# Two attentions in one program: starting with A's first group chunk by chunk, lending idle score banks, and fillers

## The chip, the cores and the metric

The kernel runs on one core of one Trainium2 chip. The metric is the device time of one execution in microseconds (us); lower is better. Engines: PE is the matmul engine (PEld its weight loads), ACT the activation engine, DVE the vector engine, POOL the general one, SP the one that issues DMA. "Span" is the time from the first to the last instruction in a trace; the timed figure of the same execution is 1.3 to 3.6 us longer in the runs here.

## The reference

Two independent attention blocks, each with 2048 rows, width 1024 and 32 heads of 32, side by side in the output.

```
A:  q, k, v = x @ wqkv ; out_A = softmax(q k^T / sqrt(32)) v @ wo          # full 2048 x 2048
B:  4 segments of 512 rows; in each: causal softmax attention inside the segment,
    plus a memory read  phi(q) M / (phi(q) z + 1e-6), mixed by g = sigmoid(beta);
    then M += phi(k)^T v, z += sum phi(k)            # phi(t) = t+1 if t>0 else exp(t)
out = concat(out_A, out_B)
```

The work comes in 8 groups of 4 heads. Per group, A has 8 items (256 queries against 2048 keys; 16 exponentials on ACT, each over two banks, 128 x 1024). B has 32 items (4 segments x 8 groups; 6 exponentials each). Together 1024 + 192 = 1216 score exponentials.

## The kernel before

A planner in Python writes every engine's instruction list at build time. It keeps an estimated clock, gives score matmuls precedence whenever score banks are free, and fits "side" work (projections, output projections, memory updates) and the multiplications by V ("PV") into the gaps of PE. The chip then runs that fixed order with semaphores. PSUM has 8 banks: 0 to 5 for scores, 6 for the PV sums, 7 for side work (6 also, until the first PV).

```
SLOTS = [(0, 1), (2, 3), (4, 5)]      # score banks in pairs
OLB = 6 ; PROJ = [7]
PACE = 200 ; LEAD = 3 ; SLOPE = 0.55  # when A's next group is prepared; when B's item is taken before A's
# ...
def loads(self):                      # B's weights and 4 tiles of B_x first
    self.load_WB(0, 0)
    for k in range(4):
        tile_in(16 + k, self.B_x[0][P * k:P * k + P, :])
        # ...
    self.load_WA(0, 0)
    for k in range(16):
        tile_in(k, self.A_x[0][P * k:P * k + P, :])
        # ...
# a_prep(g), group 0: K of all four 512-column chunks, then Q of the first, and only then scores
    for c in range(4):
        if g == 0:
            yield from self.turn([...4 tiles of x, transposed on PE, copied out by DVE and ACT in turn...])
        yield from proj(0, c)                     # K
    # ...
        yield from proj(1, 0)                     # Q of chunk 0
        # ...
        self.events.add(("sA", g, c))             # scores may start
        if c == 0:
            for v in range(4):
                yield from proj_V(v)
# schedule(): fillers on a free side bank, gap of 0.3 us, until 45 us
    if now < 45 and (RING - 1) not in self.ring_busy and not self.pos_ring and gap >= 0.3 and bank is not None:
        R.op("PE", lambda e, bank=bank: e.matmul(...), cost=MM)
```

The exponentials go to a ring of 20 tiles (10 exponentials) from which PV reads.

Of the kernel before, what the change touches and what calls it, by code (L numbers as in the profile page):

```python
# [11 lines left out]
P = 128  # L12
S = 2048
D = 1024
NI = D // P
NG = 8
# [210 lines left out]
PACE = 200  # L227
LEAD = 3
SLOPE = 0.55
STICK = True  # L230
NQ = S // 256


class Kernel:
# [69 lines left out]
    def alloc(self):  # L304
# [36 lines left out]
        self.beta = sb("beta", [P, 8])  # L341
# [28 lines left out]
    def stage(self, k):  # L370

        if k < 16:
            return self.OTA[:, k // 2, 1024 * (k % 2):1024 * (k % 2) + 1024], [("OTA", k // 2, 4 * (k % 2) + c) for c in range(4)]
        k -= 16
        flat = self.OTB[0][:, :, :].rearrange("p j n -> p (j n)")
        return flat[:, 1024 * k:1024 * k + 1024], [("OTB", 0, 2 * k), ("OTB", 0, 2 * k + 1)]

    def loads(self):
        R = self.R
        nc = self.nc  # L380

        def tile_in(k, src):
            dst, keys = self.stage(k)
            R.dma(lambda e: e.dma_start(dst, src), w=keys, issue=0.5)  # L384
        self.load_WB(0, 0)
        for k in range(4):
            tile_in(16 + k, self.B_x[0][P * k:P * k + P, :])
            if k == 1:
                self.load_WB(1, 0)
        self.events.add(("xB", 0))  # L390
        self.load_WA(0, 0)
        for k in range(16):
            tile_in(k, self.A_x[0][P * k:P * k + P, :])
            if k == 3:
                for h in range(4):
                    src = bass.AP(tensor=self.B_beta.tensor, offset=self.B_beta.offset + h, ap=[[0, 32], [4, NG]])

                    def f(e, h=h, src=src):
                        with nc.allow_non_contiguous_dma(reason="tiny beta broadcast"):
                            return e.dma_start(self.beta[32 * h:32 * h + 32, 0:NG], src)  # L400
                    R.dma(f, w=[("beta", h)], issue=0.5, mb=0.01)
            if k == 7:
                self.load_WA(1, 0)
                self.load_WB(2, 0)
        self.load_WA(2, 0)

    def late_loads(self):
        yield ("pos", 40)
        self.load_xB(1)
        self.R.dma(lambda e: e.dma_start(self.WoB[:, :, :], self.B_wo.rearrange("(j p) n -> p j n", p=P)), w=["WoB"], mb=2.0)  # L410
        self.events.add("WoB")

    def turn(self, tiles):

        R = self.R
        for n, (k, dst, dkeys) in enumerate(tiles):
            src, keys = self.stage(k)
            bank = yield ("bank",)
            yield ("pe", self.ready(keys))

            def f(e, src=src, bank=bank):
                for i in range(NI):
                    ins = e.transpose(self.psb[:, bank, P * i:P * i + P], src[:, P * i:P * i + P], self.ident[:, :])  # L423
                return ins
            R.op("PE", f, r=keys + ["ident"], w=[("ps", bank)], cost=0.9)
            pv = self.psb[:, bank, :].rearrange("p (i n) -> p i n", i=NI)
            if n % 2:
                op = R.op("ACT", lambda e, dst=dst, pv=pv: e.activation(dst, pv, ACTF.Copy), r=[("ps", bank)], w=dkeys, cost=1.1)  # L428
            else:
                op = R.op("DVE", lambda e, dst=dst, pv=pv: e.tensor_copy(dst, pv), r=[("ps", bank)], w=dkeys, cost=1.2)  # L430
            self.bank_release(bank, op)

# [29 lines left out]
    def gates(self):  # L462

        R = self.R
        rb = [("beta", h) for h in range(4)]
        gA, gB = self.gcol[:, 0, :], self.gcol[:, 1, :]
        yield ("t", max(R.lastw[k].end for k in rb) + 5.0)
        R.op("ACT", lambda e: e.activation(gB, self.beta[:, :], ACTF.Exp, scale=-1.0), r=rb, w=["gcol"], cost=0.3)
        R.op("DVE", lambda e: e.tensor_scalar(gB, gB, 1.0, None, ALU.add), r=["gcol"], w=["gcol"])
        R.op("DVE", lambda e: e.reciprocal(gA, gB), r=["gcol"], w=["gcol"])  # L470
        R.op("DVE", lambda e: e.tensor_scalar(gB, gA, -1.0, 1.0, ALU.mult, ALU.add), r=["gcol"], w=["gcol"])
        self.events.add("gates")
# [40 lines left out]
    def emit_exp(self, it, n, banks):  # L513
# [13 lines left out]
        if self.shifted and it.kind == "A":  # L527
            k = it.c // 2 if it.g == 0 else 0
            cb, ck = self.cbA[b][:, k:k + 1], [("cbA", b, k)]
        elif self.shifted:  # L530
            cb, ck = self.cbB[b][:, 0:1], [("cbB", b)]
# [192 lines left out]
    def a_prep(self, g):  # L724
# [29 lines left out]

        yield ("ev", ("WA", 0, g))
        for c in range(4):
            yield pace()
            if g == 0:
                yield from self.turn([(4 * c + t, self.xA[:, :, P * (4 * c + t):P * (4 * c + t) + P], [("xA", i, c) for i in range(NI)])
                                      for t in range(4)])  # L760
            yield from proj(0, c)
        if g + 1 < NG:
            self.load_WA(0, g + 1)
        yield ("ev", ("WA", 1, g))
        if g == 0:
            yield from proj(1, 0)
            yield from self.a_norm(g, 0, range(4), cb[:, 4:5], ("cbt", b, 0))
            for c in range(4):
                if c:
                    yield from proj(1, c)  # L770
                yield from self.a_norm(g, 1, [c], cb[:, 5 + c:6 + c], ("cbt", b, 1 + c))
                total(c)
                self.events.add(("sA", g, c))
                if c == 0:
                    yield ("ev", ("WA", 2, g))
                    for v in range(4):
                        yield from proj_V(v)
        else:
            yield from self.a_norm(g, 0, range(4), cb[:, 4:5], ("cbt", b, 0))
            for c in range(4):  # L780
                yield pace()
                yield from proj(1, c)
            yield from self.a_norm(g, 1, range(4), cb[:, 5:6], ("cbt", b, 1))
            total(0)
            for c in range(4):
                self.events.add(("sA", g, c))
            yield ("ev", ("WA", 2, g))
            for c in range(4):
                yield pace()
                yield from proj_V(c)  # L790
# [8 lines left out]
    def b_prep(self, n):  # L799
# [8 lines left out]
        if n == 0:  # L808
            yield from self.turn([(16 + t, self.xB[0][:, :, P * t:P * t + P], [("xB", 0, i) for i in range(NI)]) for t in range(4)])
# [161 lines left out]

    def ring_room(self, sizes):
        r = self.ring
        for n in sizes:
            if r + n > RING:
                r = 0
            if any((r + i) in self.ring_busy for i in range(n)):
                return False
            r += n
        return True  # L980
# [19 lines left out]
    def schedule(self):  # L1000
# [8 lines left out]
        self.banks = PROJ + [OLB]  # L1009
        self.bank_busy, self.bank_end = set(), {b: 0.0 for b in self.banks}  # L1010
        self.spawn(self.gates(), (-1, 0), "gates")
        self.spawn(self.late_loads(), (-1, 0), "loads")
        cur, nslot = None, 0
# [3 lines left out]
        while True:  # L1017
# [5 lines left out]
            while nA < 8 and (nA < 1 or ("prepA", nA - 1) in ev) and (nA < 2 or ("finA", nA - 2, NQ - 1) in ev):  # L1023
                self.spawn(self.a_prep(nA), (16 * nA - 8 if nA else 2, 2), f"prepA{nA}")
                nA += 1
            moved = True
            while moved:
                moved = False
                for t in list(self.tasks):
                    while t in self.tasks and t.req[0] != "pe" and self.satisfied(t.req, now):  # L1030
                        self.resume(t)
                        moved = True
            done = False
# [4 lines left out]
            if cur is not None:  # L1038
# [3 lines left out]
                while len(use) < GROUP and k < left:  # L1042
                    use.append(SLOTS[(nslot + len(use)) % len(SLOTS)])
                    k += len(use[-1])
                n = min(k, left)
                if self.ring_room([min(len(x), left) for x in use]):
                    end = max(self.slot_end[x] for x in use)
                    if end <= now + 0.05:
                        self.emit_scores(u, use)
                        self.run = None  # L1050
                        nslot = (nslot + len(use)) % len(SLOTS)
# [9 lines left out]
            for what in (first, "side" if first == "pv" else "pv"):  # L1061
                if done:
                    break
                if what == "pv" and self.pvq:
# [5 lines left out]
                    if v in ev and self.ready([vk]) <= now and all((st, h) in u.pend for h in range(4)) \  # L1070
# [4 lines left out]
                        if OLB in self.banks and OLB not in self.bank_busy:  # L1075
                            self.banks.remove(OLB)
                        if OLB not in self.banks:
# [16 lines left out]
            bank = next((b for b in self.banks if b not in self.bank_busy and self.bank_end[b] <= now), None)  # L1094
            if now < 45 and (RING - 1) not in self.ring_busy and not self.pos_ring and gap >= 0.3 and bank is not None:

                R.op("PE", lambda e, bank=bank: e.matmul(self.ps[:, bank, :], self.PT[:, RING - 1, 0:P], self.PT[:, RING - 1, :],
                                                             start=True, stop=True),
                     r=[("PT", RING - 1)], w=[("ps", bank)], cost=MM)
                gap = 0.0  # L1100
                continue
# [51 lines left out]
```

## Time and profile before

| | before |
|---|---|
| median of 3 runs | 1252.58 us (1246.12 to 1257.8) |
| span of the profiled run | 1254.6 us |
| ACT busy | 1134.1 us (90%) |
| PE busy | 1065.4 us (85%) |

ACT's busy time is the floor of this design, so the useful reading is: span = ACT busy + ACT idle before the stream is dense + ACT idle in the stream + tail after the last exponential. The windows view gives these pieces. Its columns: stretch, length, then busy us (instructions) of PE, PEld, DVE, ACT, POOL, then granted PE clock, DMA share, GB/s. The kernel before:

```profile
0.00:80.00 80.00, 48.81 (x314) 25.00 (x319) 24.29 (x45) 17.73 (x21) 6.67 (x20) 0.74 0.38 105
80.00:1219.70 1139.70, 996.83 (x16308) 459.68 (x16529) 759.10 (x1295) 1116.31 (x1241) 107.60 (x172) 0.95 0.22 49
1219.70:1254.60 34.90, 19.78 (x109) 7.57 (x101) 10.97 (x20) 0.02 (x1) 0.00 (x0) 0.93 0.13 48
```

ACT idles 80.00 - 17.73 = 62.3 us in the head, 23.4 us in 1139.7 us of stream, and 34.9 us in the tail. Head and tail are what can be won. Two stretches of the head, same view:

```profile
25.00:40.00 15.00, 11.71 (x46) 4.88 (x48) 2.90 (x6) 2.43 (x3) 1.34 (x2) 0.50 0.78 212
56.00:82.50 26.50, 18.38 (x80) 7.26 (x80) 3.46 (x5) 5.01 (x5) 0.00 (x0) 0.50 0.05 11
```

PE runs at half its clock there. The timeline of ACT (start, duration, engine, line, operation, count, and in brackets the idle time before and what ended it), exponentials only:

```profile
20.66 1.94 ACT L532 ACTIVATE PT<-ps 128x1024 bf16<-128x1024 f32 x2 [5.32 <-PE ps L505]
...
79.35 1.94 ACT L532 ACTIVATE PT<-ps 128x1024 bf16<-128x1024 f32 x2 [9.55 <-PE ps L505]
82.56 27.87 ACT L532 ACTIVATE PT<-ps 128x1024 bf16<-128x1024 f32 x30 [1.27 <-PE ps L505]
```

Six exponentials of B's first item come early, and the first of A at 79.35 us. In the tail, the timeline of PE:

```profile
1224.20 1.90 PE L674 MATMUL ps<-xA,OTA 128*128 128x512 bf16 x8 [1.90 <-DVE outsb L924]
1226.88 1.90 PE L674 MATMUL ps<-xA,OTA 128*128 128x512 bf16 x8 [0.79 <-DVE outsb L924]
1229.57 1.90 PE L674 MATMUL ps<-xA,OTA 128*128 128x512 bf16 x8 [0.79 <-DVE outsb L924]
```

An output projection starts every 2.69 us, for each waits until DVE has emptied the one side bank.

### The profile page before, as it was taken

To read this page: it belongs to the slowest core of one execution; us is meant where nothing else is said; L and a number is where in the kernel's file an instruction comes from. 1 tells how busy PE (TensorE), PEld (TensorE's weight loads), DVE (VectorE), ACT (ScalarE), POOL (GpSimd) and SP (SyncE) were. 2 spreads that over 40 slices of the span, in tenths; PEclk is the share of its full clock that TensorE was granted. 3 is DMA by queue.
4 is the path that set the end of the run, shared out by engine and by line. 5 is a ranking of instruction groups with operands and counts; after the bars stand their busy time and mean duration, and the time that the engine had idled before them with its cause. 6 is when DMAs were issued, how large, how long until landed. Compare 5 with 4: busy or idle time off the path is not lost.

```text
span 1254.6 us, 37128 instructions
## 1 busy us (share of the span) xinstructions
PE 1065.4 (85%) x16720; PEld 492.2 (39%) x16945; DVE 794.4 (63%) x1359; ACT 1134.1 (90%) x1261; POOL 114.3 (9%) x192
## 2 busy tenths in 40 slices
PE   5679898899888887889888887889898897889995
PEld 2334444444434333444443433334443443334442
DVE  3314846766776676776775686785676568774442
ACT  3149999999999999999999999999999999999980
POOL 2000101110101011010101020120101102010000
PEclk8769998999999988989999989889998997999999
DMA  7216122242221113313221113101221112100011
GB/s 214 46 22 165 27 58 63 53 94 56 57 52 39 33 34 65 73 27 56 57 52 31 34 33 73 39 19 44 52 57 31 31 41 84 27 19 35 36 44 44
DMA packets 195878, 66.45 MB, mean 53 GB/s; under 512 B 187008, under 2 KB 187008, under 8 KB 195712
## 3 DMA queue, kind: packets, MB, share of 16 engines
q1 hardware_dynamic: 195712, 63.99, 22.1%
q8 instruction: 135, 2.21, 0.7%
q14 instruction: 31, 0.25, 0.1%
HBM read 40.90 MB, written 8.39 MB: 39 GB/s over the span
## 4 chain that ended last, share of the span: by engine, by line
PE 46%; ACT 40%; DVE 8%; issue 3%; DMA 2%; SPq 1%; DVEq 0%
ACT PT L532 39%; PE ps L674 24%; PE ps L581 12%; PE ps L505 9%; DVE SQ L604 2%; DVE OL L591 1%; DVE outsb L924 1%; DMA out_dram<-outsb 1%; SPq L384 1%; PE ps L423 1%; ACT E L849 1%; DMA WB<-in_B_wv_dram 1%; DVE den L875 1%; ACT xA L428 0%; DVE KA L684 0%
## 5 line engine op out<-in xcount | busy, mean ns | idle before, releaser
L532 ACT ACTIVATE PT<-ps 128x1024 bf16<-128x1024 f32 (+1 forms) x1216 | 1104.0, 1040 | 43.2 <-PE ps L505 40.0
L581 PE MATMUL ps<-PT,ones 128*32 128x256 bf16 (+1 forms) x4864 | 301.5, 279 | 0.0
L581 PE MATMUL ps<-PT,VA 128*32 128x256 bf16 x4096 | 253.8, 279 | 20.1 <-ACT PT L532 15.4
L505 PE MATMUL ps<-QA,KA 32*128 32x256 bf16 x4096 | 212.0, 283 | 43.7 <-ACT PT L532 38.0
L604 DVE RECIPROCAL SQ<-OL 128x128 f32<-128x128 f32 x256 | 242.6, 948 | 4.4
L674 PE MATMUL ps<-xA,WA 128*128 128x512 bf16 x691 | 189.2, 401 | 22.6 <-issue 12.5
L674 PE MATMUL ps<-xB,WB 128*128 128x512 bf16 x692 | 182.6, 391 | 24.1 <-issue 10.8
L581 PEld LDWEIGHTS ps<-PT,VA 128*32 128x32 bf16 x4096 | 109.0, 96 | 109.7 <-issue 60.2
L505 PEld LDWEIGHTS ps<-QA,KA 32*128 32x128 bf16 x4096 | 61.6, 93 | 228.2 <-ACT PT L532 202.6
L552 POOL TENSOR_SCALAR_AFFINE_SELECT PT<-PT 128x512 bf16<-128x512 bf16 x128 | 84.3, 660 | 674.4 <-ACT PT L532 669.5
L581 PEld LDWEIGHTS ps<-PT,ones 128*32 128x32 bf16 x4864 | 133.4, 99 | 3.6
L674 PEld LDWEIGHTS ps<-xA,WA 128*128 128x128 bf16 x768 | 64.5, 101 | 105.5 <-issue 41.1
L591 DVE COPY OL<-ps 128x512 f32<-128x512 f32 x128 | 85.3, 666 | 32.4 <-PE ps L581 31.8
L674 PEld LDWEIGHTS ps<-xB,WB 128*128 128x128 bf16 x768 | 64.5, 99 | 102.8 <-issue 47.6
L924 DVE CAST outsb<-ps 128x512 bf16<-128x512 f32 x64 | 43.7, 683 | 83.4 <-PE ps L674 74.3
L875 DVE RECIPROCAL den<-den 128x128 f32<-128x128 f32 x96 | 91.1, 949 | 2.1
L684 DVE CAST KQB<-ps 128x512 bf16<-128x512 f32 x64 | 43.8, 684 | 67.5 <-PE ps L674 67.2
L674 PE MATMUL ps<-xA,OTA 128*128 128x512 bf16 x236 | 59.8, 385 | 11.9 <-DVE outsb L924 8.7
L581 PE MATMUL ps<-PT,VB 128*32 128x256 bf16 (+1 forms) x768 | 54.5, 296 | 14.4 <-DVE OL L591 10.8
L674 PE MATMUL ps<-WoB,OTB 128*128 128x512 bf16 x233 | 60.3, 381 | 4.3 <-issue 2.4
L608 DVE SCALAR_TENSOR_TENSOR OL<-OL,SQ 128x256 f32<-128x256 f32 x128 | 57.8, 451 | 2.5
L684 DVE CAST SQB<-ps 128x512 bf16<-128x512 f32 x32 | 22.0, 689 | 58.8 <-PE ps L674 58.8
(64 smaller groups left out, 497.6 us busy)
## 6 DMA issues: line engine op xcount, KB each, us to landing
WB<-in_B_wk_dram SPq DMA_DIRECT2D x32, 256.0 KB, 2.9
WB<-in_B_wq_dram SPq DMA_DIRECT2D x32, 256.0 KB, 3.0
WB<-in_B_wv_dram SPq DMA_DIRECT2D x32, 256.0 KB, 3.3
out_dram<-outsb SPq DMA_DIRECT2D x32, 256.0 KB, 2.0
WA<-in_A_wqkv_dram SPq DMA_DIRECT2D x24, 256.0 KB, 3.6
OTA<-in_A_x_dram SPq DMA_DIRECT2D x16, 256.0 KB, 5.2
WoB<-in_B_wo_dram SPq DMA_DIRECT2D x1, 2048.0 KB, 9.4
xA<-in_A_wo_dram SPq DMA_DIRECT2D x1, 2048.0 KB, 10.1
```

Source lines behind the costliest of these rows:

```text
L384: R.dma(lambda e: e.dma_start(dst, src), w=keys, issue=0.5)
L505: ins = e.matmul(o, l, r, start=True, stop=True)
L532: op = R.op("ACT", lambda e: e.activation(self.PT[:, s0:s0 + n, 0:width], self.ps[:, banks[0]:banks[0] + n, 0:width], ACTF.Exp, bias=cb, s ...
L552: mo = R.op("POOL", lambda e, ap=ap, pat=pat: e.affine_select(ap, ap, pattern=pat, compare_op=ALU.is_ge, fill=0.0, base=0, channel_multipl ...
L581: ins = e.matmul(o, l, r, start=start, stop=end, skip_group_check=True)
L591: R.op("DVE", lambda e: e.tensor_copy(self.OL[x][:, :], self.ps[:, OLB, :]), r=[("ps", OLB)], w=[("OL", x)], cost=0.66)
L604: R.op("DVE", lambda e, cs=cs: e.reciprocal(rec[:, cs], L[:, cs]), r=[ko], w=[k], cost=0.93)
L608: R.op("DVE", lambda e: e.scalar_tensor_tensor(L, L, 1.0, rec, ALU.mult, ALU.add, accum_out=self.rng[:, u.seq:u.seq + 1]), r=[k, ko], w=[k ...
L674: ins = e.matmul(o, l, rh, start=a, stop=z)
L684: op = self.R.op("DVE", lambda e: e.tensor_copy(dst, self.ps[:, bank, :]), r=[("ps", bank)], w=[dkey], cost=0.66)
L875: R.op("DVE", lambda e, cs=cs: e.reciprocal(self.den[:, cs], self.den[:, cs]), r=["den"], w=["den"], cost=0.9)
L924: op = R.op("DVE", lambda e, ns=ns, bank=bank, ob=ob: e.tensor_copy(self.outsb[ob][:, ns], self.ps[:, bank, :]), r=[("ps", bank)], w=[("ou ...
```

## The change

Intent: start A's scores as soon as one chunk of x is there, take B up after, keep PE's clock up in the head, and use score banks for side work while no scores need them. The core of the diff (evacuations, which are the copies out of PSUM by DVE or ACT, gate loading and the second, normally skipped program are cut):

```diff
-PACE = 200
-LEAD = 3
-SLOPE = 0.55
+PACE = 240
+LEAD = 0
+SLOPE = 0.65
+WARM = 60
+BLOAD = 3
@@ loads: A_x first; B's weights and x after V of A's chunk 3
+        for k in range(16):
+            tile_in(k)
+            if k == 1:
+                self.load_WA(0, 0)
+            if k == 3:
+                self.load_WA(1, 0)
+            if k == 5:
+                self.load_WA(2, 0)
+    def late_loads(self):
+        yield ("ev", ("vA", 0, BLOAD))
+        self.load_WB(0, 0)
+        self.load_xB(0)
@@ a_prep, group 0: K0, Q0, scores open, V0, K1, V1, K2, V2, K3, V3, then Q1 to Q3
+            self.events.add(("kA", g, c))
+            if early:
+                if c == 0:
+                    yield ("ev", ("WA", 1, g))
+                    yield from proj(1, 0)
+                    self.events.add(("sA", g, 0))
+                    yield ("ev", ("WA", 2, g))
+                yield from proj_V(c)
@@ schedule: banks lent at both ends
+        self.slots, self.lent = list(SLOTS[:-1]), list(SLOTS[-1])
+        self.banks = PROJ + [OLB] + self.lent
+            if self.lent and ("vA", 0, 3) in ev:      # the third score pair goes back to the scores
+                # ...
+            if self.slots and cur is None and not self.qA and not self.qB:
+                for sl in self.slots:                 # no scores left: all score banks to side work
+                    self.banks += sl
@@ schedule: fillers on any free bank, also score banks, gap 0.15 us, until 60 us
+            if now < WARM and gap >= 0.15:
+                # ... matmul of ones by ones, 512 columns
```

More of the change, by code (lines that the diff above doesn't have):

```diff
@@ L340, in alloc @@
         self.cbB = [sb(f"cbB{i}", [P, 4], F32) for i in range(2)]
-        self.beta = sb("beta", [P, 8])
+        self.beta = sb("beta", [P, 32])
         self.gcol = sb("gcol", [P, 2, 8], F32)
@@ L370, in stage, with tile_in @@
     def stage(self, k):
-        if k < 16:
-            return self.OTA[:, k // 2, 1024 * (k % 2):1024 * (k % 2) + 1024], [("OTA", k // 2, 4 * (k % 2) + c) for c in range(4)]
-        k -= 16
-        flat = self.OTB[0][:, :, :].rearrange("p j n -> p (j n)")
-        return flat[:, 1024 * k:1024 * k + 1024], [("OTB", 0, 2 * k), ("OTB", 0, 2 * k + 1)]
+        return self.OTA[:, k // 2, 1024 * (k % 2):1024 * (k % 2) + 1024], [("OTA", k // 2, 4 * (k % 2) + c) for c in range(4)]
     def loads(self):
         R = self.R
-        nc = self.nc
-        def tile_in(k, src):
+        def tile_in(k):
             dst, keys = self.stage(k)
-            R.dma(lambda e: e.dma_start(dst, src), w=keys, issue=0.5)
-        self.load_WB(0, 0)
-        for k in range(4):
-            tile_in(16 + k, self.B_x[0][P * k:P * k + P, :])
-            if k == 1:
-                self.load_WB(1, 0)
-        self.events.add(("xB", 0))
-        self.load_WA(0, 0)
-        for k in range(16):
-            tile_in(k, self.A_x[0][P * k:P * k + P, :])
-            if k == 3:
-                for h in range(4):
-                    src = bass.AP(tensor=self.B_beta.tensor, offset=self.B_beta.offset + h, ap=[[0, 32], [4, NG]])
-                    def f(e, h=h, src=src):
-                        with nc.allow_non_contiguous_dma(reason="tiny beta broadcast"):
-                            return e.dma_start(self.beta[32 * h:32 * h + 32, 0:NG], src)
-                    R.dma(f, w=[("beta", h)], issue=0.5, mb=0.01)
-            if k == 7:
-                self.load_WA(1, 0)
-                self.load_WB(2, 0)
-        self.load_WA(2, 0)
-    def late_loads(self):
+            R.dma(lambda e: e.dma_start(dst, self.A_x[0][P * k:P * k + P, :]), w=keys, issue=0.5)
+        for k in range(16):
[6 more added lines that the diff above has]
+                self.load_WA(2, 0)
+        R.dma(lambda e: e.dma_start(self.beta[0:1, :], self.B_beta.rearrange("(a n) -> a n", a=1)), w=["beta"], issue=0.5, mb=0.01)
+    def late_loads(self):
+        yield ("ev", ("vA", 0, BLOAD))
+        self.load_WB(0, 0)
+        self.load_xB(0)
+        self.load_WB(1, 0)
+        self.load_WB(2, 0)
         yield ("pos", 40)
@@ L411, in late_loads, with turn_A @@
         self.events.add("WoB")
-    def turn(self, tiles):
+    def turn_A(self):
         R = self.R
-        for n, (k, dst, dkeys) in enumerate(tiles):
+        for k in range(16):
             src, keys = self.stage(k)
+            dst, dkeys = self.xA[:, :, P * k:P * k + P], [("xA", i, k // 4) for i in range(NI)]
             bank = yield ("bank",)
@@ L424, in f @@
                 return ins
-            R.op("PE", f, r=keys + ["ident"], w=[("ps", bank)], cost=0.9)
+            R.op("PE", f, r=keys + ["ident"], w=[("ps", bank)], cost=0.6)
             pv = self.psb[:, bank, :].rearrange("p (i n) -> p i n", i=NI)
-            if n % 2:
+            if k in (1, 3):
                 op = R.op("ACT", lambda e, dst=dst, pv=pv: e.activation(dst, pv, ACTF.Copy), r=[("ps", bank)], w=dkeys, cost=1.1)
             else:
-                op = R.op("DVE", lambda e, dst=dst, pv=pv: e.tensor_copy(dst, pv), r=[("ps", bank)], w=dkeys, cost=1.2)
+                op = R.op("DVE", lambda e, dst=dst, pv=pv: e.tensor_copy(dst, pv), r=[("ps", bank)], w=dkeys, cost=0.7)
             self.bank_release(bank, op)
+            if k % 4 == 3:
+                self.events.add(("xA", k // 4))
     def constants(self):
@@ L464, in gates @@
         R = self.R
-        rb = [("beta", h) for h in range(4)]
         gA, gB = self.gcol[:, 0, :], self.gcol[:, 1, :]
-        yield ("t", max(R.lastw[k].end for k in rb) + 5.0)
-        R.op("ACT", lambda e: e.activation(gB, self.beta[:, :], ACTF.Exp, scale=-1.0), r=rb, w=["gcol"], cost=0.3)
+        yield ("t", R.lastw["beta"].end + 2.0)
+        bank = yield ("bank",)
+        yield ("pe", 0)
+        R.op("PE", lambda e: e.matmul(self.ps[:, bank, 0:32], self.ones[0:1, :], self.beta[0:1, :], start=True, stop=True),
+             r=["ones", "beta"], w=[("ps", bank)], cost=0.1)
+        for h in range(4):
+            hs = slice(32 * h, 32 * h + 32)
+            src = self.ps[hs, bank, 0:32].rearrange("p (j h) -> p j h", h=4)[:, :, h]
+            op = R.op("ACT", lambda e, hs=hs, src=src: e.activation(self.gcol[hs, 1, :], src, ACTF.Exp, scale=-1.0),
+                      r=[("ps", bank)], w=["gcol"], cost=0.2)
+        self.bank_release(bank, op)
         R.op("DVE", lambda e: e.tensor_scalar(gB, gB, 1.0, None, ALU.add), r=["gcol"], w=["gcol"])
@@ L527, in emit_exp @@
         if self.shifted and it.kind == "A":
-            k = it.c // 2 if it.g == 0 else 0
-            cb, ck = self.cbA[b][:, k:k + 1], [("cbA", b, k)]
+            cb, ck = self.cbA[b][:, 0:1], [("cbA", b, 0)]
         elif self.shifted:
@@ L753, in total @@
                  r=[("cbt", b, 0), ("cbt", b, 1 + k)], w=[("cbA", b, k)], cost=0.1)
+        early = g == 0 and not self.shifted
         yield ("ev", ("WA", 0, g))
@@ L758, in a_prep @@
             if g == 0:
-                yield from self.turn([(4 * c + t, self.xA[:, :, P * (4 * c + t):P * (4 * c + t) + P], [("xA", i, c) for i in range(NI)])
-                                      for t in range(4)])
+                yield ("ev", ("xA", c))
             yield from proj(0, c)
+            self.events.add(("kA", g, c))
[6 more added lines that the diff above has]
+                yield from proj_V(c)
         if g + 1 < NG:
@@ L764, in a_prep @@
         yield ("ev", ("WA", 1, g))
-        if g == 0:
-            yield from proj(1, 0)
-            yield from self.a_norm(g, 0, range(4), cb[:, 4:5], ("cbt", b, 0))
-            for c in range(4):
-                if c:
-                    yield from proj(1, c)
-                yield from self.a_norm(g, 1, [c], cb[:, 5 + c:6 + c], ("cbt", b, 1 + c))
-                total(c)
-                self.events.add(("sA", g, c))
-                if c == 0:
-                    yield ("ev", ("WA", 2, g))
-                    for v in range(4):
-                        yield from proj_V(v)
-        else:
-            yield from self.a_norm(g, 0, range(4), cb[:, 4:5], ("cbt", b, 0))
-            for c in range(4):
-                yield pace()
-                yield from proj(1, c)
-            yield from self.a_norm(g, 1, range(4), cb[:, 5:6], ("cbt", b, 1))
-            total(0)
-            for c in range(4):
-                self.events.add(("sA", g, c))
-            yield ("ev", ("WA", 2, g))
-            for c in range(4):
-                yield pace()
-                yield from proj_V(c)
+        yield from self.a_norm(g, 0, range(4), cb[:, 4:5], ("cbt", b, 0))
+        for c in range(1 if early else 0, 4):
+            yield pace()
+            yield from proj(1, c)
+            if not self.shifted:
+                self.events.add(("sA", g, c))
+        yield from self.a_norm(g, 1, range(4), cb[:, 5:6], ("cbt", b, 1))
+        total(0)
+        for c in range(4):
+            self.events.add(("sA", g, c))
+        yield ("ev", ("WA", 2, g))
+        for c in range(0 if not early else 4, 4):
+            yield pace()
+            yield from proj_V(c)
         if g + 1 < NG:
@@ L807, in b_prep @@
         yield ("ev", ("xB", s))
-        if n == 0:
-            yield from self.turn([(16 + t, self.xB[0][:, :, P * t:P * t + P], [("xB", 0, i) for i in range(NI)]) for t in range(4)])
         for k in range(2):
@@ L970, in resume, with keys_ready @@
             self.tasks.remove(task)
+    def keys_ready(self, it, n):
+        return it.kind == "B" or all(("kA", it.g, u.steps[st][part][0] // 4) in self.events
+                                     for u, st, _ in it.slots[it.scored:it.scored + n] for part in range(2))
     def ring_room(self, sizes):
@@ L1008, in schedule @@
         self.slot_end = {s: 0.0 for s in SLOTS}
-        self.banks = PROJ + [OLB]
+        self.slots, self.lent = list(SLOTS[:-1]), list(SLOTS[-1])
+        self.banks = PROJ + [OLB] + self.lent
         self.bank_busy, self.bank_end = set(), {b: 0.0 for b in self.banks}
@@ L1012, in schedule @@
         self.spawn(self.late_loads(), (-1, 0), "loads")
+        self.spawn(self.turn_A(), (-1, 1), "turnA")
         cur, nslot = None, 0
@@ L1023, in schedule @@
             while nA < 8 and (nA < 1 or ("prepA", nA - 1) in ev) and (nA < 2 or ("finA", nA - 2, NQ - 1) in ev):
-                self.spawn(self.a_prep(nA), (16 * nA - 8 if nA else 2, 2), f"prepA{nA}")
+                self.spawn(self.a_prep(nA), (16 * nA - 8 if nA else -1, 2), f"prepA{nA}")
                 nA += 1
@@ L1032, in schedule @@
                         moved = True
+            if OLB in self.banks and (("vA", 0, 0) in ev or ("vB", 0) in ev):
+                self.banks.remove(OLB)
+            if self.lent and ("vA", 0, 3) in ev:
+                self.banks = [b for b in self.banks if b not in self.lent]
+                if not self.bank_busy & set(self.lent) and nslot == 0:
+                    self.slots.append(SLOTS[-1])
+                    self.slot_end[SLOTS[-1]] = max(self.bank_end[b] for b in self.lent)
+                    self.lent = []
+            if self.slots and cur is None and not self.qA and not self.qB:
+                for sl in self.slots:
+                    self.banks += sl
+                    for b in sl:
+                        self.bank_end[b] = self.slot_end[sl]
+                self.slots = []
             done = False
@@ L1041, in schedule @@
                 use, k = [], 0
-                while len(use) < GROUP and k < left:
-                    use.append(SLOTS[(nslot + len(use)) % len(SLOTS)])
+                while len(use) < (GROUP if len(self.slots) > 2 else 1) and k < left:
+                    use.append(self.slots[(nslot + len(use)) % len(self.slots)])
                     k += len(use[-1])
                 n = min(k, left)
-                if self.ring_room([min(len(x), left) for x in use]):
+                if self.ring_room([min(len(x), left) for x in use]) and self.keys_ready(u, n):
                     end = max(self.slot_end[x] for x in use)
@@ L1050, in schedule @@
                         self.run = None
-                        nslot = (nslot + len(use)) % len(SLOTS)
+                        nslot = (nslot + len(use)) % len(self.slots)
                         if u.scored == len(u.slots):
@@ L1074, in schedule @@
                             and (c <= room or len(self.ring_busy) > RING - 4):
-                        if OLB in self.banks and OLB not in self.bank_busy:
-                            self.banks.remove(OLB)
-                        if OLB not in self.banks:
+                        if OLB not in self.bank_busy:
                             self.emit_pv(u, st, part)
@@ L1093, in schedule @@
                 break
-            bank = next((b for b in self.banks if b not in self.bank_busy and self.bank_end[b] <= now), None)
-            if now < 45 and (RING - 1) not in self.ring_busy and not self.pos_ring and gap >= 0.3 and bank is not None:
-                R.op("PE", lambda e, bank=bank: e.matmul(self.ps[:, bank, :], self.PT[:, RING - 1, 0:P], self.PT[:, RING - 1, :],
-                                                             start=True, stop=True),
-                     r=[("PT", RING - 1)], w=[("ps", bank)], cost=MM)
-                gap = 0.0
-                continue
+            if now < WARM and gap >= 0.15:
+                spare = [b for b in self.banks if b not in self.bank_busy and self.bank_end[b] <= now]
+                if self.slots and self.slot_end[self.slots[nslot]] <= now:
+                    spare.append(self.slots[nslot][0])
+                spare = [b for b in spare if self.ready([("ps", b), "ones"]) + LAT <= now]
+                if spare:
+                    R.op("PE", lambda e, bank=spare[0]: e.matmul(self.ps[:, bank, :], self.ones[:, :], self.ones[:, :].unsqueeze(1).to_broadcast([P, 4, P]),
+                                                                 start=True, stop=True), r=["ones"], w=[("ps", spare[0])], cost=MM)
+                    gap = 0.0
+                    continue
             R.free["PE"] = now + 0.05
```

## The prediction

> **What bounds the kernel now.** Three stages (windows view and timeline of before).
>
> 1. Head, 0 to 82.5 us. Only 8 of 1216 score exponentials on ACT fall here; ACT is under 30% busy. The chain of waits runs through the PE: transposes and projections, one bank at a time (transposes wait for evacuations, 0.69 us on DVE or 1.02 us on ACT). From 25 to 40 and 56 to 80 us the granted clock is 0.50: eight transposes take 1.03 us instead of 0.62, a projection 3.6 instead of 1.9 us. The first A scores come at 78.7 us, after all K chunks and Q0.
> 2. Stream, 82.5 to 1219.7 us. ACT is busy 1115 of 1137 us: 1208 exponentials (about 0.90 us of busy time each) and the E activations of B. PE waits for ACT 76 us. ACT bounds.
> 3. Tail, 1219.7 to 1254.6 us. No exponentials; ten output projections through a single bank, one every 2.69 us, 0.79 us of it waiting for the evacuation.
>
> **What the change does.**
> Head: x comes first, and the first scores need 4 tiles, 2 weights, K0 and Q0. Four banks take transposes, not two. Loads: 19 x 256 KB = 5.0 MB; at the 250 to 300 GB/s seen in the busy stretches of the head, an estimate of 20 to 22 us for all and about 8 us for chunk 0. PE per chunk, warm: 4 x 0.62 + 2 x 1.9 = 6.3 us, plus Q0 once: about 27 us of PE after the first tile at 4.7 us. So I expect first scores at 13 to 16 us, four exponentials per key chunk, K3 ready at 32 to 36 us, and ACT above 90% from there. With 12 exponentials done by then, the effective start of the stream is about 24 us, against 82.5 - 7 = 75 us. Gain about 51 us.
> Fillers keep the clock up: the Trainium skill, "TensorE: Matmul & The Clock Gate", Part 1, says that half rate is the default and that a busy window of about 3.4 us gives full rate; the trace shows both rates (1.03 and 0.62 us).
> Stream: ACT work is unchanged. B0's and B1's projections (6 x 1.9 us and their memory update) move from the head into it, into PE slack. I allow 22 to 30 us of ACT idle. Slope, lead and pace: a few us either way.
> Tail: with the score banks lent the projections run at about 1.9 us: ten save 8 us. A larger backlog takes some of that back. I expect 27 to 34 us.
>
> **Sum.** 24 (effective start) + 1096 (exponentials) + 28 (E) + 25 (idle) + 30 (tail) = 1203 us, range 1185 to 1222. The head gain is all critical: ACT has no slack to catch up. Chances: faster by over 2% 0.92, same 0.07, slower 0.01.
>
> **What would show each step.** First exponential with KA before 18 us; ACT tenths of 9 from about 35 us; granted clock near 1 from 8 to 60 us; ACT idle in the stream 22 to 30 us; last exponential near 1170 us; tail projections 1.9 us apart.
>
> **What would make it wrong.** Fillers that run out before late data, so the clock falls back to half (head 10 us longer); V's transposed loads stuck behind x in the queue, so that the ring fills and exponentials stop; side work short of PE time, so B's items lag and stand alone at the end, with ACT waiting (10 to 30 us longer).

## The result

| | before | after |
|---|---|---|
| median | 1254.62 us (4 runs) | 1202.7 us (4 runs, 1201.71 to 1203.76) |
| ratio | | 0.9597, interval 0.9546 to 0.9647 |
| span of the profiled run | 1254.6 | 1198.7 |
| ACT busy | 1134.1 | 1125.4 |
| ACT idle, 0 to 80 us | 62.3 | 27.3 |
| ACT idle, 80 us to last exponential | 23.4 | 15.5 |
| tail | 34.9 | 30.5 |

The differences of the lower four rows, 8.7 + 35.0 + 7.9 + 4.4 = 56.0 us, are the difference of the spans. The 8.7 us of ACT work are mostly the copies of x: ACT did ten (1.02 us each) and does two. All ten lay in the first 70 us, where ACT was mostly waiting, so this item belongs to the head, which makes 43.7 of the 56.0 us. The differences add up to more than the timed gain (about 50 us by the ratio), because the profiled run of before was one of the longer ones: 1256.35 us, 3.8 us above the median of its first three runs.

The windows view of the changed kernel:

```profile
0.00:80.00 80.00, 70.78 (x855) 32.73 (x870) 31.11 (x52) 52.72 (x61) 4.06 (x16) 1.00 0.58 149
80.00:1168.20 1088.20, 951.89 (x15740) 440.35 (x15944) 761.25 (x1293) 1072.66 (x1196) 112.39 (x176) 0.97 0.22 49
1168.20:1198.70 30.50, 19.80 (x117) 8.78 (x117) 11.09 (x20) 0.03 (x1) 0.00 (x0) 0.87 0.15 55
```

The clock in the head reads 1.00 now. The lengths of eight transposes in PE's timeline show that it is full only from about 7 us on (before that the column is wrong, see the end):

```profile
3.79 1.03 PE L414 MATMUL ps<-ident,OTA 128*128 128x128 bf16 x8 [0.19 <-DMA OTA<-in_A_x_dram]
...
7.45 0.61 PE L414 MATMUL ps<-ident,OTA 128*128 128x128 bf16 x8
```

The timeline of ACT, exponentials:

```profile
15.99 3.77 ACT L532 ACTIVATE PT<-ps 128x1024 bf16<-128x1024 f32 x4 [6.09 <-PE ps L506]
26.70 3.83 ACT L532 ACTIVATE PT<-ps 128x1024 bf16<-128x1024 f32 x4 [2.25 <-PE ps L506]
33.49 3.77 ACT L532 ACTIVATE PT<-ps 128x1024 bf16<-128x1024 f32 x4 [2.97 <-PE ps L506]
39.80 9.27 ACT L532 ACTIVATE PT<-ps 128x1024 bf16<-128x1024 f32 x10 [2.53 <-PE ps L506]
```

Four exponentials follow each chunk of K, and from 39.80 us ACT is nearly dense. The tail, timeline of PE (PV between the first two lines left out):

```profile
1166.10 12.03 PE L674 MATMUL ps<-xA,OTA 128*128 128x512 bf16 x54 [0.16 <-issue]
...
1183.04 1.14 PE L674 MATMUL ps<-xA,OTA 128*128 128x512 bf16 x4 [3.70 <-DVE OTA L612]
1184.39 7.41 PE L674 MATMUL ps<-xA,OTA 128*128 128x512 bf16 x27 [0.22 <-issue]
```

The projections now follow each other without the 0.79 us. But a new wait of 3.70 us has appeared. The last item's PV stands behind those 54 matmuls and ends at 1179.3 us; PE has then nothing to do until DVE has divided that item. Before, this PV ran at once and its division was hidden behind projections of older items.

### The profile page after: what moved, and what is told of

It is laid out like the page before. It is cut to its first block, busy times and chain, and to the rows that moved or that the text cites. A ratio compares the mean times of both kernels' runs of the same rounds, so it can differ in the third digit from the quotient of the medians.

```text
span 1198.7 us, 37080 instructions
## 1 busy us (share of the span) xinstructions
PE 1042.5 (87%) x16699; PEld 481.9 (40%) x16927; DVE 803.4 (67%) x1363; ACT 1125.4 (94%) x1256; POOL 116.5 (10%) x192
## 4 chain that ended last, share of the span: by engine, by line
ACT 47%; PE 40%; DVE 10%; issue 3%; DMA 1%; SPq 0%; DVEq 0%
ACT PT L532 46%; PE ps L674 21%; PE ps L581 9%; PE ps L506 8%; DVE SQ L604 2%; DVE OL L591 2%; DVE den L870 1%; ACT E L844 1%; DVE OL L608 1%; DVE amem L877 1%; DMA OTA<-in_A_x_dram 1%; DVE OTA L612 0%; DVE den L864 0%; DVE outsb L919 0%; DMA out_dram<-outsb 0%
## 5 line engine op out<-in xcount | busy, mean ns | idle before, releaser
L581 PE MATMUL ps<-PT,ones 128*32 128x256 bf16 (+1 forms) x4864 | 295.6, 275 | 0.0
L674 PE MATMUL ps<-xB,WB 128*128 128x512 bf16 x684 | 179.2, 383 | 21.2 <-issue 11.6
L674 PE MATMUL ps<-xA,WA 128*128 128x512 bf16 x695 | 181.6, 387 | 16.5 <-issue 8.7
L674 PEld LDWEIGHTS ps<-xB,WB 128*128 128x128 bf16 x768 | 61.8, 98 | 95.2 <-issue 45.3
L684 DVE CAST KQB<-ps 128x512 bf16<-128x512 f32 x64 | 43.7, 683 | 57.8 <-PE ps L674 57.4
L581 PE MATMUL ps<-PT,VB 128*32 128x256 bf16 (+1 forms) x768 | 50.8, 282 | 15.3 <-DVE OL L591 12.0
L684 DVE CAST VT<-ps 128x512 bf16<-128x512 f32 x32 | 22.0, 687 | 47.7 <-PE ps L674 44.3
```

The lines of the kernel that those rows point to most:

```text
L581: ins = e.matmul(o, l, r, start=start, stop=end, skip_group_check=True)
L674: ins = e.matmul(o, l, rh, start=a, stop=z)
L684: op = self.R.op("DVE", lambda e: e.tensor_copy(dst, self.ps[:, bank, :]), r=[("ps", bank)], w=[dkey], cost=0.66)
```

## The experiments

My theory after reading the traces: the order of work gives most of the gain, lending the rest of the head and the tail, and the fillers about 10 us by keeping the clock up. The main rival: the head of before was long because PE ran at half rate, so fillers and clock are the change. Twelve kernels ran, all correct. They ran in four batches on four chips, each with the kernel before beside it (its medians: 1250.67 to 1254.01 us), so times are best compared by the ratio. For each, the pieces as in the table above, in lost us of ACT. They come from the profiled run alone, which was often the fastest of its kernel: below the median by 9.4 us in a_nofill_p216, 4.6 in a_order, 3.9 in a_both and at most 2.7 in the others.

| run | median us | ratio to before | span | idle 0-80 | idle in stream | tail |
|---|---|---|---|---|---|---|
| changed kernel | 1202.7 | 0.9597 | 1198.7 | 27.3 | 15.5 | 30.5 |
| a_nofill | 1217.33 | 0.9731 | 1213.0 | 27.5 | 29.7 | 29.9 |
| a_tiny | 1204.15 | 0.9612 | 1201.8 | 28.4 | 17.5 | 30.6 |
| a_nofill_p216 | 1216.41 | 0.9714 | 1204.6 | 28.2 | 19.7 | 30.8 |
| a_nohead | 1217.49 | 0.973 | 1213.1 | 28.1 | 27.4 | 31.5 |
| a_notail | 1206.11 | 0.9636 | 1201.9 | 26.9 | 16.0 | 33.7 |
| a_oldpar | 1215.51 | 0.9718 | 1212.3 | 27.0 | 26.4 | 33.3 |
| a_order | 1225.63 | 0.9808 | 1219.1 | 33.2 | 25.4 | 35.2 |
| b_fill | 1241.14 | 0.9926 | 1239.2 | 51.9 | 20.7 | 33.9 |
| b_fill_lend | 1244.47 | 0.9955 | 1241.9 | 44.8 | 36.3 | 26.2 |
| a_tailpv | 1196.36 | 0.955 | 1194.1 | 27.2 | 16.5 | 25.0 |
| a_kfirst | 1216.02 | 0.9704 | 1210.7 | 32.7 | 24.1 | 28.5 |
| a_both | 1211.79 | 0.9672 | 1205.1 | 32.6 | 22.1 | 25.2 |

### a_nofill, and a_tiny: what are the fillers worth?

Edit of a_nofill:

```diff
-WARM = 60
+WARM = 0
```

> The changed kernel with no filler matmuls at all. Theory (order of the work is the main thing, the clock second): the first chunks run at half rate, first score exponential at 18 to 21 us instead of 16.0, K3 scores 5 to 12 us later than 39.4, time 1207 to 1216 us. Rival (the head of before was long because the PE ran at half rate, so the fillers are the change): the head falls back most of the way, time above 1230 us.

Measured: 1217.33 us, 15 us slower than the changed kernel, just above the range of the theory; but not where either theory put it. The first exponential comes at 17.09 us instead of 15.99, and up to 80 us ACT loses only 0.2 us more. The stream loses 14.2 us more. A comparison of the two programs shows why that can be: without fillers, the planner's clock differs from the start, and it writes another order on every engine, far beyond the head. So this run does not measure the fillers alone. I therefore kept the order, and shrank the fillers:

```diff
-e.matmul(self.ps[:, bank, :], self.ones[:, :], self.ones[:, :].unsqueeze(1).to_broadcast([P, 4, P]),
+e.matmul(self.ps[:, bank, 0:1], self.ones[:, :], self.ones[:, 0:1],
```

> The changed kernel in exactly its own order of instructions on every engine; only the 13 fillers, all before 9 us, shrink from 512 columns to 1, so that they do no work. Theory: taking the fillers away cost 14 us because it changed the whole static order after it, not because of the clock; so here the head is 0 to 3 us longer, the stream as in the changed kernel (ACT idle 15 to 20 us), time 1200 to 1206 us. Rival (the fillers' clock is worth the 14 us): 1213 us or more.

Measured: 1204.15 us, ratio 0.9612 against 0.9597. The order on every engine is that of the changed kernel. ACT's exponentials in the head, same view as above:

```profile
17.11 3.77 ACT L532 ACTIVATE PT<-ps 128x1024 bf16<-128x1024 f32 x4 [7.38 <-PE ps L506]
...
40.91 9.27 ACT L532 ACTIVATE PT<-ps 128x1024 bf16<-128x1024 f32 x10 [2.53 <-PE ps L506]
```

Up to 52 us all of ACT's exponentials are 1.1 us later; the stream of this one trace then loses 2.0 us more. By the timed runs the work of the fillers is worth 1 to 2 us. There are only 13 of them, all before 9 us. Without their work PE reaches the full rate a little later, by about 13 us, as its projections of eight matmuls show:

```profile
10.04 3.22 PE L674 MATMUL ps<-xA,WA 128*128 128x512 bf16 x8
...
14.00 1.89 PE L674 MATMUL ps<-xA,WA 128*128 128x512 bf16 x8
```

The rival falls, and so does my own size of 10 us.

### a_nofill_p216: does another pace bring the 14 us back?

```diff
 # a_nofill, and
-PACE = 240
+PACE = 216
```

> No fillers, as in the run that cost 14 us, but with pace 216 instead of 240, a value for which the kernel's own planner finds a schedule with as little planned idle of ACT as that of the changed kernel. Theory: pace 240 fits one particular order, and a pace fitted anew brings most of the 14 us back: time 1202 to 1209 us, ACT idle in the stream 16 to 23 us. Rival (fillers matter by themselves): 1213 us or more.

Measured: the profiled run took 1206.97 us with 19.7 us idle in the stream, as expected. The other six runs took 1214.65 to 1217.6 us. Their granted clock was 0.950 to 0.953, that of the profiled run 0.966. So the expectation of the theory failed by the median, and its trace shows the exception. What the six have in common is only that clock; they have no trace. The fast run is also the profiled one; whether that matters, no run tests. See below.

### a_nohead and a_notail: the two ends of the lending

```diff
 # a_nohead
-        self.slots, self.lent = list(SLOTS[:-1]), list(SLOTS[-1])
+        self.slots, self.lent = list(SLOTS), []
 # a_notail
-            if self.slots and cur is None and not self.qA and not self.qB:
+            if False:
```

> The changed kernel with the third pair of score banks not lent to side work in the head (two banks for transposes and projections, as before; score pairs 3 from the start). Theory: transposes wait for evacuations again, K3 scores 3 to 8 us later than 39.4, time 1205 to 1211 us. Rival (banks are the main gain of the head): 1220 us or more.

> The changed kernel with the score banks not lent after the last scores. Theory: the last exponential stays near 1168 us and the remaining 9 to 10 output projections come 2.69 us apart instead of 1.73, so the tail is 5 to 8 us longer than 30.5: time 1208 to 1211 us. Rival (the last attention output bounds the tail, not the bank): within 2 us of the changed kernel.

a_nohead: 1217.49 us, outside both ranges. The first exponential comes at 23.68 us instead of 15.99, and those of K3 at 42.84 instead of 39.80, 3.0 us later, as the theory said. But the gaps after that are shorter, so that up to 80 us ACT loses only 0.8 us more than in the changed kernel. In the stream it loses 11.9 us more. So by 80 us the lent pair has won next to nothing. The loss lies in the stream, where the planner has written another order again.

a_notail: 1206.11 us, a smaller effect than expected. Up to the last exponential the loss of ACT agrees with the changed kernel within 0.5 us, and the tail is 3.2 us longer; by the timed ratios the lending is worth (0.9636 - 0.9597) x 1252 = 5 us, though the two intervals overlap. This ablation is clean: in the built programs ACT's list is the same as in the changed kernel, and the other lists part only at the end. The effect is small because in a_notail the last PV starts at once, at 1167.67 us, so the wait of 3.70 us is missing too: the lending wins more and gives these 3.7 us back. Its PE in the tail has the old rhythm:

```profile
1174.25 1.90 PE L674 MATMUL ps<-xA,OTA 128*128 128x512 bf16 x8 [0.79 <-DVE outsb L919]
1176.94 1.90 PE L674 MATMUL ps<-xA,OTA 128*128 128x512 bf16 x8 [0.79 <-DVE outsb L919]
```

### a_oldpar: the three numbers

```diff
-PACE = 240
-LEAD = 0
-SLOPE = 0.65
+PACE = 200
+LEAD = 3
+SLOPE = 0.55
```

> The changed kernel with the old slope, lead and pace (0.55, 3, 200). Theory: these only move B against A; ACT idle in the stream 17 to 28 us (18.7 now), time 1200 to 1210 us. Rival (the new numbers are needed, since with the old ones B lags and stands alone at the end): 1215 us or more with ACT idle late in the stream.

Measured: 1215.51 us; the theory's range is exceeded by 5 us, and the time lies in the rival's. The head is the same, the stream loses 10.9 us more and the tail 2.8 us more. But the rival's reason fails too: B does not stand alone at the end (its last scores come before 1100 us, as in the changed kernel), and the loss is spread over the stream. A comparison of built programs narrows it down: with only slope and lead set back, the program is the same as that of the changed kernel, byte for byte; with only the pace set back, it is that of a_oldpar. So of the three numbers only the pace acts here.

### a_order, b_fill and b_fill_lend: the order against the rest

a_order is the changed kernel with the edits of a_nofill, a_nohead, a_notail and a_oldpar together. b_fill is the kernel before with the filler block of the change and `WARM = 90`. b_fill_lend adds the bank lending at both ends.

> Only the order: x of A first, chunk by chunk, B after; no fillers, no lending at either end, old parameters. Theory: the head gain remains but for 8 to 18 us, the tail gain goes: time 1217 to 1232 us, thus about half of the whole gain or more. Rival: over 1240 us.

> The kernel before with the fillers of the change (on free score banks too, gap 0.15 us, until 90 us); order, banks and parameters as before. Theory (order): the clock in the head is near 1, so the 55 us of it that ran at half rate shorten by 10 to 20 us, first A scores at 60 to 68 us instead of 78.7, time 1234 to 1245 us. Rival (clock is the main thing): gain over 35 us, time below 1220 us.

> The kernel before with everything of the change but the order of loads and work and the three parameters: fillers, and banks lent at both ends. Theory: on top of the fillers the tail loses 5 to 8 us and the head a few; time 1222 to 1236 us, so at least 20 us of the gain remain for the order. Rival (order matters little): below 1212 us.

The order alone: 1225.63 us, a gain of 24 us (0.0192 x 1252; interval of the ratio 0.9782 to 0.9833) out of 50. Its windows view of the head:

```profile
0.00:80.00 80.00, 60.39 (x784) 30.85 (x793) 31.51 (x54) 46.78 (x55) 4.06 (x16) 1.00 0.58 150
```

ACT loses 33.2 us there, against 62.3 before and 27.3 in the full change, so 29.1 of the 35.0 us won in the head. "Order" still holds small things that no run tests alone: most copies of x moved from ACT to DVE, another loading of the gates, and other cost estimates in the planner. Fillers put into the kernel before: 1241.14 us, a gain of 9 us (interval 0.9896 to 0.9955); the first A exponential comes at 69.08 us. The first scores are a little later than the theory said, the time is in its range, and far from the rival's. Fillers and lending without the order: 1244.47 us, no better than fillers alone (the intervals overlap) and outside both ranges. There the lending wins 7.1 us in the first 80 us and 7.7 us in the tail, as it should; but after 80 us the stream loses 15.6 us more. Of this, 12.9 us lie before 200 us (14.8 us idle there against 1.9 in b_fill), one gap of 10.76 us before 86.16 us among them: the head has been stretched, not shortened.

So the rival falls for good: the order is needed, and neither clock nor banks replace it. But the parts don't add up: 24 us and 6 us (0.0045 x 1252) make 30, not 50. From a_order to the full change the spans differ by 20.4 us: 5.9 us in the head, 9.9 in the stream, 4.7 in the tail. Neither a_order nor b_fill_lend has the new pace, and a_oldpar, which lacks only that, loses as much in the stream as a_order (26.4 and 25.4 us).

### a_tailpv, a_kfirst and a_both: can it be improved?

a_tailpv gives PV precedence once the score banks are lent out at the end:

```diff
-            first = self.run if STICK and self.run else ("pv" if full else "side")
+            first = "pv" if not self.slots else self.run if STICK and self.run else ("pv" if full else "side")
```

> The changed kernel, with the last attention output multiplied before side work once the score banks are lent out. In the changed kernel the last 40 of these matmuls start only at 1178.1 us, 10 us after the last exponential, behind 6 output projections, and PE then idles 3.7 us for the division of that item. Theory: this idle time goes, last exponential unchanged near 1168 us, tail 26 to 28 us instead of 30.5, time 1198 to 1200.5 us. Rival (the tail is bound by the PE's projections alone): within 1 us of the changed kernel.

Measured: 1196.36 us, ratio 0.955, interval 0.9526 to 0.9573. It was compared with the kernel before in its own rounds, not with the changed kernel; through that common base it is 0.5% faster than the changed kernel. The two intervals overlap, so the time alone doesn't show it; but all its runs (1195.01 to 1198.47 us) are below all of the changed kernel, and the trace shows the wait gone. Here too the built programs differ only at the end. The tail is 25.0 us, 5.5 us shorter, a little more than the 3.7 us of the wait; PE's timeline shows the rest of the backlog in one piece:

```profile
1169.87 17.44 PE L674 MATMUL ps<-xA,OTA 128*128 128x512 bf16 x80
1188.48 0.18 PE L648 MATMUL ps<-Mb,ones 128*128 128x1 bf16 x1 [1.17 <-DVE Mb L646]
```

a_kfirst changes two things at once: it projects K of the next chunk before V of the last, and puts the transposes behind the projections:

```diff
-                yield from proj_V(c)
+                else:
+                    yield from proj_V(c - 1)
+                if c == 3:
+                    yield from proj_V(c)
-        self.spawn(self.turn_A(), (-1, 1), "turnA")
+        self.spawn(self.turn_A(), (-1, 3), "turnA")
```

> The changed kernel, with K of the next chunk projected before V of the last, and transposes of later tiles behind projections. Theory: the gap of ACT from 19.8 to 26.7 us shrinks by 4 us or more, but what counts is when K3 is there, since 12 exponentials precede it either way: it comes 1 to 3 us earlier (one projection of 1.9 us moved behind it), time 1199 to 1202 us. Rival (the gaps of ACT count each by itself): 5 us or more off, 1196 us or less.

> Both of the last two together. Theory: the gains add, time 1195 to 1199 us.

a_kfirst: 1216.02 us, slower by 13 us, against both theories. Its ACT timeline:

```profile
14.81 3.77 ACT L532 ACTIVATE PT<-ps 128x1024 bf16<-128x1024 f32 x4 [4.98 <-PE ps L506]
21.65 3.83 ACT L532 ACTIVATE PT<-ps 128x1024 bf16<-128x1024 f32 x4 [3.07 <-PE ps L506]
31.86 3.77 ACT L532 ACTIVATE PT<-ps 128x1024 bf16<-128x1024 f32 x4 [5.73 <-PE ps L506]
41.22 5.61 ACT L532 ACTIVATE PT<-ps 128x1024 bf16<-128x1024 f32 x6 [5.59 <-PE ps L506]
```

The second chunk does come 5 us earlier. But the delayed transposes then stand in the way: each later chunk waits for transposes, their evacuation and the projection in sequence, K3's scores come 1.4 us later than in the changed kernel, and the delayed work makes another gap of 6.37 us before 53.20 us. This is 5.4 us up to 80 us; another 8.6 us are lost in the stream. So I read the early transposes, which looked like the cause of the gap from 19.8 to 26.7 us, as what keeps the later chunks on time; no run delays them alone. a_both, 1211.79 us, has the head of a_kfirst and the tail of a_tailpv (25.2 us), so those two pieces are independent; as a prediction of time it failed with a_kfirst.

### The half-rate spells in the stream

a_nofill, a_nohead, a_oldpar and a_kfirst differ from the changed kernel by one part, three of them by a part of the head, and lose 8.6 to 14.2 us more in the stream. A look at the granted clock in steps of 2 us shows where some of it goes. One spell in the changed kernel, windows view:

```profile
420.00:422.00 2.00, 1.13 (x32) 0.61 (x36) 1.88 (x3) 2.00 (x3) 0.00 (x0) 1.00 0.36 69
422.00:424.00 2.00, 1.43 (x32) 0.69 (x28) 1.93 (x3) 2.00 (x4) 1.37 (x3) 0.67 0.00 0
424.00:426.00 2.00, 1.63 (x32) 0.63 (x28) 1.73 (x5) 1.98 (x3) 1.38 (x2) 0.50 0.00 0
...
428.00:430.00 2.00, 1.41 (x24) 0.54 (x28) 1.93 (x5) 1.53 (x3) 1.91 (x3) 0.50 0.00 0
...
438.00:440.00 2.00, 1.84 (x26) 0.82 (x16) 1.90 (x5) 2.00 (x4) 0.00 (x0) 1.00 0.55 127
```

The clock falls to 0.50 during 422 to 424 us, in the middle of a B item's scores. ACT still has work from its banks; its first idle time (2.00 - 1.53 us) comes 4 us later, in 428 to 430 us. So the slow PE comes first and the idle ACT after. Matmuls in PE's timeline just before and just inside:

```profile
421.78 0.29 PE L581 MATMUL ps<-PT,VB 128*32 128x256 bf16 x4 [0.57 <-ACT PT L532]
...
424.44 0.41 PE L581 MATMUL ps<-PT,VB 128*32 128x256 bf16 x4
```

Counted over all steps of 2 us from 80 to 1160 us, those with a clock under 0.9 and ACT's idle time in them:

| run (profiled) | us with clock under 0.9 | ACT idle in these | ACT idle in the others |
|---|---|---|---|
| before | 130 | 15.3 | 7.6 |
| changed kernel | 80 | 7.2 | 8.2 |
| a_tiny | 88 | 9.4 | 8.0 |
| a_nofill_p216 | 80 | 9.5 | 10.1 |
| a_oldpar | 94 | 15.4 | 10.9 |
| a_nohead | 98 | 14.9 | 12.4 |
| a_kfirst | 98 | 14.1 | 10.0 |
| a_nofill | 102 | 19.0 | 10.6 |

The spells take 7 to 12% of the stream, and hold about half to two thirds of ACT's idle time there. Of the 7.5 us less idle between before and after in this stretch, all lies in them (15.3 to 7.2). Of the runs not in the table, b_fill_lend does not fit: it has 130 us of low clock, as before, with 13.8 us of idle time in the spells and 21.1 outside. So the spells are not the whole story of the stream. This is a count on single traces, and it goes together; no run here takes the spells away by themselves, so how much of the time is caused by them is argued, not shown. One thing more goes with them: in the changed kernel PE was busy for 1.69 to 2.80 us of the 4 us before each of its nine spells (in the steps at a higher clock it is busy 88% on average). But 30 other stretches of 4 us (taken every 2 us) with as little work had no spell after them, so this alone doesn't start one. The a_nofill_p216 runs fit: same program, clock 0.966 with 1207 us, 0.95 with 1215 to 1218 us.

## Why the prediction was right or wrong

The time was predicted as 1203 us and measured as 1202.7. That it fits so closely is luck: the stream started 4.4 us later than predicted, its exponentials took 2.8 us less and its idle time 6.4 us less, and the sum left out that the timed figure is a few us above the span. In terms of the trace:

| term | predicted | measured |
|---|---|---|
| effective start of the stream | 24 | 39.8 - 11.4 (busy time of the 12 exponentials before) = 28.4 |
| exponentials and E of B | 1096 + 28 = 1124 | 1109.8 from 39.8 us on, + 11.4 before = 1121.2 |
| ACT idle in the stream (from 39.8 us) | 25 | 1128.4 - 1109.8 = 18.6 |
| tail | 30 | 30.5 |
| sum | 1203 | 1198.7 (the span; timed 1201.71) |

- The head's mechanism was right: first scores at 15.6 us (13 to 16 predicted), four exponentials per chunk, clock near 1 from 8 us on. Its size was off: K3's scores came at 39.4 us, not 32 to 36. The mis-sized term is "PE per chunk, warm": 27 us of PE from the first tile on, counting transposes and projections only. That work held its estimate: from 3.8 to 39.4 us PE spent 10.0 us on transposes and 14.6 us on projections, together 24.6. But it also spent 3.6 us on scores, 1.7 us on PV and 3.2 us on fillers (these overlap a little: 30.8 us busy in all), and it idled 4.8 us, mostly behind evacuations. Those were left out. The loads were not the limit: DMA moved nothing from 18 to 20 us. The gain in effective start was 75.6 - 28.4 = 47 us instead of 51.
- Fillers: the warning "head 10 us longer" without the clock was mis-sized. They are worth 1 to 2 us in this order (a_tiny). The quoted page was read correctly, but what followed from it was not: PE's own work brings the full rate by about 13 us without them. The Trainium skill, "TensorE: Matmul & The Clock Gate", Part 1, gives about 3.4 us of activity for full rate. In the changed kernel PE starts at 1.72 us, and eight transposes take 1.03 us at 3.79 us and 0.61 us at 7.45 us, which fits. a_tiny fits less well: there PE was busy for 4.89 of the 6.44 us before 10.04 us, almost all of it with transposes, and the eight at 9.22 us still took 1.03 us. What counts as activity these runs don't settle.
- Stream: "a few us either way" for slope, lead and pace failed. The old values cost about 14 us of idle time and tail by the traces (10.9 + 2.8), and only the pace is behind it (a_oldpar and the comparison of programs). "22 to 30 us of ACT idle" failed downward by 3 to 11 us. a_nofill, a_nohead and a_kfirst, which re-order the head, lose 24 to 30 us there again, with the same pace. So I read the short stream of the changed kernel as a good fit of the pace to this one order, not as a consequence of the new head; a_nofill_p216 shows that fitting the pace anew does not bring it back reliably. B's side work moved into the stream, whose idle time still fell (23.4 to 15.5 us after 80 us).
- Tail: size right (30.5 against 27 to 34), and its projections 1.7 us apart where they run on. The reason for its not being shorter was wrong. I named a larger backlog; about ten projections remain, as before, and the rest is the new 3.70 us wait behind the delayed PV, which a_tailpv takes away.

What stays open: what exactly starts a half-rate spell, and how much of the stream's differences would go if none came.

## What to carry to other kernels

Where one engine is the floor, split the span into its busy time, its idle time at the start, in the stream, and at the end. Then judge each part of a change in its own piece. In a kernel whose whole instruction order comes from one planner, taking a small part away re-orders everything behind it, so an ablation is only clean if the order is kept (fillers of 1 column instead of none: 1 to 2 us instead of 15). When idle resources are lent to side work, check that the side work does not overtake the one step that the end depends on.

## What the Trainium skill lacked or had wrong

- The Trainium skill, "TensorE: Matmul & The Clock Gate", section "Why this matters for your kernels", advises no PE-idle gaps over about 3 us to avoid throughput drops. Here the clock fell to 0.50 with no such gap: PE's longest wait between 408 us and the spell at 422 us was 1.23 us, and in 420 to 422 us it was busy for 1.13 of 2.00 us. That section lacks the case of a PE that never rests for long but is busy only about half the time, here with matmuls of 32 rows or 32 columns. Another section of the page, "A second HAM failure mode: psum-queue depth-cycling", does tell of a clock that swings because PE rests briefly and often, but gives no share of busy time for it.
- The same page says in Part 1 that the clock events of a trace have been seen to be unreliable, so this is nothing that it lacks. This trace agrees: the clock column reads 1.00 from 0 to 14 us in the changed kernel, while eight transposes took 1.03 us at 3.79 us and 0.61 us at 7.45 us.
- No page says that the same program can run at a mean clock of 0.966 in one execution and 0.950 to 0.953 in the six others, with 1207 us and 1215 to 1218 us (a_nofill_p216). What Part 1 of the same page tells of differences between runs is about the warm-up only.
